# Operands moved by 32 bytes, queue orders and buffers changed, the last inverse transform in steps of two pairs: a spectral layer with a feed-forward network

## The chip, the cores and the metric

The kernel runs on one core of a Trainium2 chip. TensorE (PE) multiplies matrices; its weight loads (PEld) are shown apart. VectorE (DVE), ScalarE (ACT) and GpSimd (POOL) work elementwise, and SyncE (SP) issues the DMAs. TensorE writes into PSUM, which has eight banks; all else lies in SBUF, at a byte offset that is the same in each of 128 partitions. The metric is device time of one execution in microseconds (us); smaller is better.

## The reference

A spectral layer over 8 sequences of 3008 rows and 256 channels, then a two-layer network on all 24064 rows:

```python
def _attn_ref(x, w_r, w_i, b_r, b_i):
    X = np.fft.rfft(x, axis=1)
    Xr, Xi = X.real, X.imag
    Yr = Xr @ w_r - Xi @ w_i + b_r
    Yi = Xr @ w_i + Xi @ w_r + b_i
    Yr = np.sign(Yr) * np.maximum(np.abs(Yr) - lam, 0.0)     # lam = 0.01
    Yi = np.sign(Yi) * np.maximum(np.abs(Yi) - lam, 0.0)
    return np.fft.irfft(Yr + 1j * Yi, n=x.shape[1], axis=1)

def _moe_ref(x, w_in, w_out):        # x: 24064 x 256, w_in: 256 x 2048, w_out: 2048 x 256
    h = x @ w_in
    return (h - np.tanh(h)) @ w_out
```

## The kernel before

**The mathematics.** The transform of 3008 = 64 x 47 points is split: a DFT over 47 points (class `Forward`, L216 to L218), one over 64 points (`Spectrum`, L262), the linear layer (L289, products `ps_t` and `ps_v`), the shrinking step, an inverse over 64 points (L336 to L338), and an inverse over 47 points (class `Unit`, L428), which gives the rows of the network's input in `raw`. A sequence has 32 pairs of residues; a pair becomes 94 rows. Values are kept as a high and a low part (`x_h`, `x_l`) in a rounded 32-bit format, and a product is three matmuls: high by low, high by high, low by high. `split_into` makes the parts: ScalarE casts the high one (L87) and GpSimd, or VectorE at the start, subtracts (L88). The matmuls of L262 and L428 take plain 32-bit operands, and the profile shows each as two records.

**The network.** The rows are cut into 48 chunks of 512 or 480 columns. Chunks 0 to 2 (`Chunk.up`, L481, and `Chunk.down`, L505) run while the weights are still being unpacked. From chunk 3 on, `Pair` makes two blocks of 128 hidden units at a time with seven half-size products instead of eight (L576, three matmuls each, 256 or 240 columns), from operands `y_...` and from weights `win` or sums of weights `sum...`; between the products ScalarE copies (L584, L585) and VectorE adds (L592 `u3`, L598 `low_right`). Then come tanh (L607), the difference (L610), the high part `gh` (L614) and the low part `gl` (L618), and the down-projection, L505: twelve matmuls a pair with `wout` as weights and `gh`, `gl` as the moving operand, 512 or 480 columns wide. One pair is two slots of the plan.

**What sets the order.** The order on each engine is written out by hand. `plan()` puts each piece of spectral work into a slot with a rank; `run(slot)` issues a slot's pieces by rank. DFT over 64 points: rank 6; `shared` and `cross` products: 4 and 3; shrinking and inverse: 2; the split of x: 2, one slot ahead of `Forward.part`, which is rank 7; the operands of the next chunk (four of them in the third slot before it): 1; a `Unit` step: 8; weight sums and sums of operands: 9. Engines then run their own queue strictly in this order and wait for each other by semaphores. Work of VectorE and GpSimd that follows a piece is returned by it and issued a little later (`run_later`).

**Buffers.** Spectral work of the main loop shares two PSUM banks (`ps_ff`, in `bank()`). A `Unit` loads up to three pairs, and `time(t)` multiplies them for one half `t` of the channels into one bank and copies it out: four steps a chunk. A chunk's first rows may belong to the unit of the chunk before; they wait in `spill` until `unspill`. `weight_sums` makes the sums of weights in four steps on VectorE, in three small tiles `ws0` to `ws2`, from which ScalarE and GpSimd split them; it runs at slots 36 to 53, where the early chunks end and the pairs begin. Before the loop the pools `ps_h`, `ps_o` and `ps_f` hold eight banks; they are closed, and `ps_oo`, `ps_ff` and `ps_e` take them.

**Places.** A partition's offsets are given out in order of the pools and tags. The tile `shifts` (two columns, for two constants of activations) and what lies around it leave every later tile at byte 32 of a 64-byte block, `gh`, `gl`, `th`, `x_h`, `x_l`, `z_h`, `z_l`, `raw` and the `y` operands among them; `win` and `wout`, ahead of it, are at multiples of 64.

## Time and profile before

| | |
|---|---|
| median of three runs | 2660.9 us (2659.74 to 2662.64) |
| the profiled execution's own time | 2656.65 us |
| its span, first to last instruction | 2654.8 us |
| mean granted clock of TensorE | 0.994 |
| DMA | 163.90 MB, mean 62 GB/s |

The profile is of one execution. A row of the timeline has start and length in us, engine, line, operation, out<-in, shape, and in brackets the idle time before it with what ended it. A row of a group has the count after x, then busy us, mean ns of one, and idle us before them with their releasers. Matmuls are pipelined: a matmul's length is longer than the distance to the next one's start, so the pace is read from starts. A row of windows has the stretch and its length, busy us of the engine, the granted clock, and the DMA share. Idle time of an engine that nobody waits for costs nothing.

### The profile page before, as it was taken

How to read it: one execution, taken by the hardware profiler on the slowest of the kernel's cores; microseconds unless marked ns; L12 is line 12 of the kernel's file. 1: busy time of each engine (PE TensorE's matmuls, PEld its weight loads, DVE VectorE, ACT ScalarE, POOL GpSimd, SP SyncE). 2: the span in 40 equal slices, each digit the busy share in tenths (PEclk: the TensorE clock that was granted, in tenths of full speed). 3: DMA queues.
4: the chain of work that ended last, by engine and by line, in shares of the span. 5: the costliest groups of instructions: out<-in, count | busy, mean ns of one | idle time of the engine just before them, and what ended most of it. 6: DMA issues, size and time to landing. Idle time of an engine off the chain costs nothing.

```text
span 2654.8 us, 43312 instructions
## 1 busy us (share of the span) xinstructions
PE 2611.6 (98%) x16641; PEld 2343.2 (88%) x16641; DVE 1720.6 (65%) x2613; ACT 1578.9 (59%) x2950; POOL 697.9 (26%) x829
## 2 busy tenths in 40 slices
PE   8999999999999999999999999999999999999999
PEld 6787788899989999899998999989999899999998
DVE  6787676576656667466664666646665566665655
ACT  5555656655566555755566555665556655555555
POOL 0002524322242222512334232332223322221210
PEclk8899999999999999999999999999999999999999
DMA  6420313211131111311114011231112211111000
GB/s 195 149 76 14 110 59 102 70 40 53 38 111 55 47 50 40 106 59 40 45 49 125 29 54 38 73 95 41 43 52 84 68 46 55 36 33 33 16 24 16
DMA packets 104654, 163.90 MB, mean 62 GB/s; under 512 B 8000, under 2 KB 62272, under 8 KB 104352
## 3 DMA queue, kind: packets, MB, share of 16 engines
q1 hardware_dynamic: 104448, 161.13, 19.7%
q8 instruction: 132, 2.16, 0.3%
q14 instruction: 74, 0.61, 0.1%
HBM read 86.13 MB, written 74.97 MB: 61 GB/s over the span
## 4 chain that ended last, share of the span: by engine, by line
PE 86%; DVE 2%; POOL 1%; ACT 1%; issue 1%; DMA 0%; SPq 0%; POOLq 0%; ACTq 0%; DVEq 0%
PE o L505 36%; PE H L576 32%; PE ps_v L289 4%; PE ps_i L428 4%; PE ps_f L262 3%; PE ps_t L289 2%; PE ps_f L218 1%; PE ps_f L216 1%; PE ps_f L217 1%; DVE y L326 1%; PE ps_i L336 1%; PE ps_i L337 1%; PE ps_i L338 1%; POOL x_l L88 1%; DVE tb L300 0%
## 5 line engine op out<-in xcount | busy, mean ns | idle before, releaser
L576 PEld LDWEIGHTS H<-y_t,sum 128*128 128x128 f32 x3240 | 530.6, 188 | 91.8 <-DVE H L592 3.9
L505 PE MATMUL o<-gh,wout_l 128*128 128x512 f32 (+1 forms) x1440 | 572.5, 398 | 0.1
L505 PE MATMUL o<-gh,wout_h 128*128 128x512 f32 (+1 forms) x1440 | 561.5, 390 | 0.0
L505 PE MATMUL o<-gl,wout_h 128*128 128x512 f32 (+1 forms) x1440 | 560.7, 389 | 0.5 <-DVE gl L618 0.5
L576 PE MATMUL H<-y_t,sum 128*128 128x256 f32 (+1 forms) x3240 | 550.9, 278 | 4.1 <-DVE H L592 3.5
L614 ACT CAST gh<-th 128x1024 fp32r<-128x1024 f32 (+1 forms) x360 | 372.3, 1034 | 281.1 <-DVE th L610 231.4
L618 DVE TENSOR_TENSOR gl<-th,gh 128x1024 fp32r<-128x1024 f32 (+1 forms) x360 | 435.7, 1210 | 48.8 <-ACT gh L614 44.1
L592 DVE TENSOR_TENSOR H<-H,late 128x256 f32<-128x256 f32 (+1 forms) x360 | 153.6, 427 | 450.5 <-PE H L576 407.7
L610 DVE TENSOR_TENSOR th<-H,th 128x1024 f32<-128x1024 f32 (+1 forms) x360 | 429.3, 1192 | 2.4 <-ACT th L607 0.3
L607 ACT ACTIVATE th<-H 128x1024 f32<-128x1024 f32 (+1 forms) x360 | 364.6, 1013 | 108.8 <-PE H L576 105.7
L505 PEld LDWEIGHTS o<-gl,wout_h 128*128 128x128 f32 x1440 | 270.3, 188 | 56.1 <-DVE gl L618 0.9
L88 POOL TENSOR_TENSOR z_l<-mn,z_h 128x512 fp32r<-128x512 f32 x84 | 110.3, 1313 | 769.3 <-ACT z_h L87 769.3
L598 DVE TENSOR_TENSOR H<-H,late 128x256 f32<-128x256 f32 (+1 forms) x360 | 153.6, 427 | 242.1 <-PE H L576 235.7
L576 PE MATMUL H<-y_b,win_h 128*128 128x256 f32 (+1 forms) x1440 | 284.7, 279 | 0.0
L505 PEld LDWEIGHTS o<-gh,wout_l 128*128 128x128 f32 x1440 | 272.1, 189 | 6.8 <-ACT gh L614 0.5
L505 PEld LDWEIGHTS o<-gh,wout_h 128*128 128x128 f32 x1440 | 272.0, 189 | 5.7
L584 ACT COPY late<-H 128x256 f32<-128x256 f32 (+1 forms) x360 | 132.8, 369 | 235.5 <-PE H L576 232.6
L576 PE MATMUL H<-y_more,win_h 128*128 128x256 f32 (+1 forms) x1440 | 266.5, 278 | 0.0
L576 PEld LDWEIGHTS H<-y_more,win_h 128*128 128x128 f32 x1440 | 219.0, 189 | 4.4
L576 PEld LDWEIGHTS H<-y_b,win_h 128*128 128x128 f32 x1440 | 219.6, 189 | 0.0
L576 PE MATMUL H<-y_more,win_l 128*128 128x256 f32 (+1 forms) x720 | 209.3, 291 | 0.0
L576 PE MATMUL H<-y_b,win_l 128*128 128x256 f32 (+1 forms) x720 | 200.8, 279 | 0.0
(173 smaller groups left out, 4213.6 us busy)
## 6 DMA issues: line engine op xcount, KB each, us to landing
xt<-in_x SPq DMA_DIRECT2D x64, 384.0 KB, 3.8
at<-a SPq DMA_DIRECT2D x96, 256.0 KB, 3.2
z<-zo SPq DMA_DIRECT2D x96, 256.0 KB, 2.1
a<-st SPq DMA_DIRECT2D x56, 384.0 KB, 3.4
zin<-z SPq DMA_DIRECT2D x58, 288.0 KB, 3.8
out<-ot SPq DMA_DIRECT2D x32, 512.0 KB, 3.1
out<-ot SPq DMA_DIRECT2D x16, 480.0 KB, 3.4
zin<-z SPq DMA_DIRECT2D x31, 192.0 KB, 3.6
```

The source lines that it names most:

```text
L88: rest.tensor_tensor(out=lo, in0=src, in1=hi.bitcast(F32), op=ALU.subtract)
L289: nc.tensor.matmul(dst, lhs[:, t], rhs[:, t, :], start=n == 0, stop=n == 5)
L428: nc.tensor.matmul(ps[:, k * 94:(k + 1) * 94], self.zt[:, k, t * P:(t + 1) * P], i2t[:, (self.p + k) * 94:(self.p + k + 1) * 94], start=Tr ...
L505: nc.tensor.matmul(self.o[t][:, :n], lhs[:, f, t * P:(t + 1) * P], rhs, start=f == 0 and k == 0, stop=f == NF - 1 and k == 2,)
L576: nc.tensor.matmul(dst, a, b, start=start and k == 0, stop=k == 2, skip_group_check=True)
L584: nc.scalar.copy(out=self.p7, in_=self.c11)
L592: nc.vector.tensor_tensor(out=self.c21, in0=self.acc, in1=self.p7, op=ALU.add)
L598: nc.vector.tensor_tensor(out=self.c22, in0=self.acc, in1=self.p7, op=ALU.add)
L607: nc.scalar.activation(out=self.th, in_=self.hp[:, :, :n], func=AF.Tanh)
L610: nc.vector.tensor_tensor(out=self.th, in0=self.hp[:, :, :self.n], in1=self.th, op=ALU.subtract)
L614: nc.scalar.copy(out=self.gh, in_=self.th)
L618: nc.vector.tensor_tensor(out=self.gl, in0=self.th, in1=h(self.gh), op=ALU.subtract)
```

## The change

**Places.** The tile `shifts` becomes `below` with one column; `rebias` is made later, by GpSimd instead of VectorE, as a tile of the pool `work` of its own, just ahead of the tag `ot`. All tiles from `ot` on move up by 32 bytes, to multiples of 64: `gh`, `gl`, `th`, `raw`, `st`, and the tiles of `x_h`, `x_l`, `z_h`, `z_l`, `xh`, `xl`, `s_h`. What lies ahead of it stays: the `y` operands, `sum...`, `at`, `zin`, the constants.

**Queue orders.** The split of x goes from rank 2 to 0.5, ahead of the operands. The inverse over 64 points goes from rank 2 to 2.5, and to 6.5 where its slot holds a DFT (6) and nothing of ranks 3, 4, 7, 8. `Unit` steps are placed by `unit_slots`, first into slots whose only spectral work is a DFT. And the memory of `rebias` is set on GpSimd.

**Buffers.** `weight_sums` has two tiles with two parts each: steps three and four put the second sum into a fourth part instead of overwriting one that is being split. The PSUM pools open in the order `ps_f`, `ps_h`, `ps_o`, so that the early chunks' pool `ps_e` takes the banks of `ps_h` and `ps_o` instead of those of `ps_f`; and `ps_e` waits tile by tile for the banks' last users.

**Units.** A unit loads up to four pairs, and `both(k)` does two pairs for both halves into one bank, with one copy for both: three steps a chunk instead of four. The matmuls are the same in number and shape.

```diff
+    ps_f = start.enter_context(tc.tile_pool(name="ps_f", bufs=4, space=PSUM))
     ps_h = start.enter_context(tc.tile_pool(name="ps_h", bufs=2, space=PSUM))
     ps_o = start.enter_context(tc.tile_pool(name="ps_o", bufs=1, space=PSUM))
-    ps_f = start.enter_context(tc.tile_pool(name="ps_f", bufs=4, space=PSUM))
...
-                self.zt = work.tile([96, 3, D], F32, name="zin", tag=tag, bufs=1)
+                self.zt = work.tile([96, 4, D], F32, name="zin", tag=tag, bufs=1)
...
-        def multiply(self, ps, t):
-            for k in range(self.n):
+        def multiply(self, ps, t, at=0, which=None):
+            for j, k in enumerate(which or range(self.n)):
...
+        def both(self, k):
+            ps = bank("ps_i2")
+            m = min(2, self.n - k)
+            n = m * 94
+            for t in range(2):
+                self.multiply(ps, t, t * n, range(k, k + m))
+            pv = ps[:, :2 * n].rearrange("p (t n) -> p t n", t=2)
+            for chunk, at, cols in self.pieces(k, m):
+                chunk.take_both(at, pv[:, :, cols])
...
+        def take_both(self, at, src):
+            nc.scalar.copy(out=self.home(at, src.shape[2]), in_=src)
...
-        t = [work.tile([P, 2, P], F32, name=f"ws{k}", tag="tmp", bufs=4) for k in range(3)]
+        pair = [work.tile([P, 2, 2, P], F32, name=f"ws{k}", tag="tmp", bufs=4) for k in range(2)]
+        t = [v[:, k] for v in pair for k in range(2)]
...
         def three():
             put_sum(0, t[1])
-            op(t[1], t[1], t[2], ALU.subtract)
+            op(t[3], t[1], t[2], ALU.subtract)
             whole(t[2], 1, 0)
 
         def four():
-            put_sum(1, t[1])
-            op(t[2], t[2], t[1], ALU.subtract)
+            put_sum(1, t[3])
+            op(t[2], t[2], t[3], ALU.subtract)
...
     def run(slot):
-        for _, _, fn, a in sorted(slots.pop(slot, []), key=lambda e: e[:2]):
+        events = slots.pop(slot, [])
+        ranks = {e[0] for e in events}
+        if ranks >= {2.5, 6} and not ranks & {3, 4, 7, 8}:
+            events = [(6.5, *e[1:]) if e[0] == 2.5 else e for e in events]
+        for _, _, fn, a in sorted(events, key=lambda e: e[:2]):
...
-                (k + shrink, 2, lambda s=s: [s.shrink], 0.3), (k + inverse, 2, s.inverse, 0.7),
+                (k + shrink, 2, lambda s=s: [s.shrink], 0.3), (k + inverse, 2.5, s.inverse, 0.7),
...
-        put(slot - 1, 2, f.split, q)
+        put(slot - 1, 0.5, f.split, q)
...
-            at = (zs - 8, zs - 7, zs - 6, zs - 6) if c == WB_N else calmest(zs - 10 if i == 0 else zs - 14, zs - 6, 4, 0.7)
-            for k, (p, n) in enumerate(((lo, 3), (lo + 3, hi - lo - 3))):
+            at = unit_slots(c, (hi - lo + 1) // 2)
+            for p, first in ((lo, 0), (lo + 4, 2)):
...
+                put(max(at[first] - 5, done_at.get(b, 0) + 1, last_two[-3] + 1), 0, u.load)
+                for k in range(0, n, 2):
+                    put(at[first + k // 2], 8, u.both, k)
...
+        alone = [k for k in range(lo, hi + 1) if {e[0] for e in slots.get(k, ())} & {2, 2.5, 3, 4, 6, 7} == {6}]
+        found = alone[:n]
...
-        shifts = const.tile([P, 2], F32, name="shifts")
-        below, rebias = shifts[:, 0:1], shifts[:, 1:2]
+        below = const.tile([P, 1], F32, name="below")
         nc.vector.memset(below, -LAM)
-        nc.vector.memset(rebias, -896.0)
...
+        rebias = work.tile([P, 1], F32, name="rebias", bufs=1)
+        nc.gpsimd.memset(rebias, -896.0)
...
-        ps_e = first_pass.enter_context(tc.tile_pool(name="ps_e", bufs=1, space=PSUM))
+        ps_e = first_pass.enter_context(tc.tile_pool(name="ps_e", bufs=1, space=PSUM, reuse_waits="tile"))
```

What it does to three queues. First GpSimd, three slots before a chunk from one of the later sequences begins: `y_t` and `y_b` are low parts of the chunk's operands, `x_6_0_l` that of the sixth forward piece, `late` and `raw` sums of operands. Before:

```order
L531 TENSOR_TENSOR late<-raw 128x256
L531 TENSOR_TENSOR raw<-raw 128x256
L531 TENSOR_TENSOR late<-raw 128x256
L88 TENSOR_TENSOR y_t_1981<-late,y_t_1981 128x256
L88 TENSOR_TENSOR y_b_1982<-raw,y_b_1982 128x256
L88 TENSOR_TENSOR y_t_1984<-late,y_t_1984 128x256
L88 TENSOR_TENSOR y_b_1983<-raw,y_b_1983 128x256
L88 TENSOR_TENSOR x_6_0_l<-xt,x_6_0_h 94x512
```

And now:

```order
L550 TENSOR_TENSOR late<-raw 128x256
L550 TENSOR_TENSOR raw<-raw 128x256
L550 TENSOR_TENSOR late<-raw 128x256
L88 TENSOR_TENSOR x_6_0_l<-xt,x_6_0_h 94x512
L88 TENSOR_TENSOR y_t_1980<-late,y_t_1980 128x256
L88 TENSOR_TENSOR y_b_1981<-raw,y_b_1981 128x256
L88 TENSOR_TENSOR y_t_1983<-late,y_t_1983 128x256
L88 TENSOR_TENSOR y_b_1982<-raw,y_b_1982 128x256
```

The split of x stands ahead of the four operands now; the casts on ScalarE move in the same way.

Second TensorE, in a slot of the second sequence's spectra (`z_6` goes through the inverse, `at` through the DFT; `H` belongs to the pair that the slot lies in). Before:

```order
L576 MATMUL H_2036<-y_b_1982,win_h 128x240 x2
L336 MATMUL ps_i_3381<-z_6_h,i_l 128x512
L337 MATMUL ps_i_3381<-z_6_h,i_h 128x512
L338 MATMUL ps_i_3381<-z_6_l,i_h 128x512
L262 MATMUL ps_f_3388<-f_126,at 128x2x64 x4
L576 MATMUL H_2035<-y_more,win_l 128x240
```

And now:

```order
L595 MATMUL H_2035<-y_b_1981,win_h 128x240 x2
L262 MATMUL ps_f_3373<-f_125,at 128x2x64 x4
L336 MATMUL ps_i_3383<-z_6_h,i_l 128x512
L337 MATMUL ps_i_3383<-z_6_h,i_h 128x512
L338 MATMUL ps_i_3383<-z_6_l,i_h 128x512
L595 MATMUL H_2034<-y_more,win_l 128x240
```

The DFT goes ahead of the inverse in seven of the ten slots that hold both; the other three hold a `Unit` step too.

Third VectorE, in a round of weight sums (`the`, `gle` and `he` belong to the early chunks). Before, step three overwrites `ws1`, which GpSimd is reading:

```order
L631 TENSOR_TENSOR ws1_1850<-ws0_1849,ws1_1850 128x256
L631 TENSOR_TENSOR ws0_1849<-ws2_1851,ws0_1849 128x256
L490 TENSOR_TENSOR gle_1058<-the_1054,ghe_1056 128x512
L485 TENSOR_TENSOR the_1053<-he0_1049,the_1053 128x512
L631 TENSOR_TENSOR ws1_1850<-ws1_1850,ws2_1851 128x256
L628 TENSOR_TENSOR ws2_1851<-win_h_78,win_l_79 128x256
```

And now it writes the second part of `ws1` while the second part of `ws0` is read:

```order
L651 TENSOR_TENSOR ws0_1850<-ws0_1850 128x256
L651 TENSOR_TENSOR ws0_1850<-ws1_1851,ws0_1850 128x256
L509 TENSOR_TENSOR gle_1059<-the_1055,ghe_1057 128x512
L504 TENSOR_TENSOR the_1054<-he0_1050,the_1054 128x512
L651 TENSOR_TENSOR ws1_1851<-ws0_1850,ws1_1851 128x256
L648 TENSOR_TENSOR ws1_1851<-win_h_78,win_l_79 128x256
```

The order is the same; the buffers differ, and with them what has to be waited for.

More of the change, by code (lines that the diff above doesn't have):

```diff
@@ L438, in take @@
                 end = min(hi, begin[c] + sizes[c])
-                src = ps[:, lo - self.b * S - self.p * 94:end - self.b * S - self.p * 94]
-                chunks[c].take(t, lo - begin[c], src, c)
+                yield chunks[c], lo - begin[c], slice(lo - first, end - first)
                 lo = end
+        def take(self, ps, t):
+            for chunk, at, cols in self.pieces():
+                chunk.take(t, at, ps[:, cols])
+        def both(self, k):
[7 more added lines that the diff above has]
+                chunk.take_both(at, pv[:, :, cols])
     Unit.turn = 0
@@ L456, in open, with take @@
                 )
-        def take(self, t, at, src, c):
+        def take(self, t, at, src):
             n = src.shape[1]
@@ L763, in plan, with unit_slots @@
             zs = zero_slot(c)
-            at = (zs - 8, zs - 7, zs - 6, zs - 6) if c == WB_N else calmest(zs - 10 if i == 0 else zs - 14, zs - 6, 4, 0.7)
-            for k, (p, n) in enumerate(((lo, 3), (lo + 3, hi - lo - 3))):
-                u = Unit(b, p, n)
-                put(max(at[2 * k] - 4 + k, done_at.get(b, 0) + 1), 0, u.load)
-                for t in range(2):
-                    put(at[2 * k + t], 8, u.time, t)
+            at = unit_slots(c, (hi - lo + 1) // 2)
+            for p, first in ((lo, 0), (lo + 4, 2)):
+                n = min(4, hi - p)
+                if n <= 0:
+                    continue
+                u = Unit(b, p, n)
+                last_two.append(at[first + (n - 1) // 2])
+                put(max(at[first] - 5, done_at.get(b, 0) + 1, last_two[-3] + 1), 0, u.load)
+                for k in range(0, n, 2):
+                    put(at[first + k // 2], 8, u.both, k)
+    last_two = [0, 0]
+    def unit_slots(c, n):
+        zs = zero_slot(c)
+        if c == WB_N:
+            return (zs - 8, zs - 7, zs - 6)
+        lo, hi = (zs - 10 if c % WB_N == 0 else zs - 14), zs - 6
+        alone = [k for k in range(lo, hi + 1) if {e[0] for e in slots.get(k, ())} & {2, 2.5, 3, 4, 6, 7} == {6}]
+        found = alone[:n]
+        rest = [k for k in range(lo, hi + 1) if k not in found]
+        found = sorted(found + sorted(rest, key=lambda k: (load_at.get(k, 0.0), k))[:n - len(found)])
+        for k in found:
+            busy(k, 0.9)
+        return found
     wsteps = {}
```

22 lines of the change are left out of this document (12 added, 10 removed).

## The prediction

> **What bounds the kernel now.** I read the page first, for the engine that sets the end, then the chain of work, then the matmuls grouped by shape, then the list of waits, and last the timeline at the places where TensorE waits.
>
> ```profile
> span 2654.8 us, 43312 instructions
> PE 2611.6 (98%) x16641; PEld 2343.2 (88%) x16641; DVE 1720.6 (65%) x2613; ACT 1578.9 (59%) x2950; POOL 697.9 (26%) x829
> ...
> PE 86%; DVE 2%; POOL 1%; ACT 1%; issue 1%; DMA 0%; SPq 0%; POOLq 0%; ACTq 0%; DVEq 0%
> ```
>
> TensorE (PE) is busy 98% of the span, and 86% of the chain that ended last is its own matmuls; no other engine passes 65%. So two things can shorten the span: matmuls that follow each other faster, and TensorE's waits, 2654.8 - 2611.6 = 43 us in all. The list of waits says for whom:
>
> ```profile
> PE ps_f L218 <- POOL x_l L88: 9.8, 7, 1.6
> PE ps_f L262 <- DVE y L326: 7.2, 10, 0.7
> PE H L576 <- DVE H L592: 3.5, 1, 3.5
> ...
> PE H L481 <- DVE the L485: 1.7, 1, 1.7
> PE he L481 <- DVE yl L462: 1.6, 1, 1.6
> ...
> PE H L576 <- POOL y_b L88: 0.7, 1, 0.7
> ```
>
> Columns: us in total, times, longest. These six rows are 24.5 us, and each is touched by an edit. Busy time says little of how fast matmuls follow each other, since they overlap; that is read from their starts, in steps of the timeline where nothing waits:
>
> ```profile
> 1.91 5.06 PE L815 MATMUL idle<-warm 128*128 128x512 f32 x11 [1.91 <-DVE shifts L821]
> ...
> 105.44 1.99 PE L815 MATMUL idle<-warm 128*128 128x512 f32 x8
> ...
> 1108.84 0.38 PE L505 MATMUL o<-gh,wout_l 128*128 128x480 f32 x1
> ...
> 1110.16 0.50 PE L576 MATMUL H<-y_t,sum 128*128 128x240 f32 x3
> ...
> 2408.44 0.40 PE L505 MATMUL o<-gh,wout_l 128*128 128x512 f32 x1
> ...
> 2409.84 0.52 PE L576 MATMUL H<-y_t,sum 128*128 128x256 f32 x3
> ```
>
> Between the two rows at 2408.44 and 2409.84 stand six L505 matmuls of 512 columns: 1.40 / 6 = 0.233 us each. With 480 columns, from 1108.84 to 1110.16, it is 1.32 / 6 = 0.220. The eight idle matmuls at 105.44, one set of weights and nothing accumulated, take (1.99 - 0.40) / 7 = 0.227. The eleven at 1.91, at half the granted clock, take (5.06 - 0.79) / 10 = 0.427, if their last runs twice 0.40 (the same 0.43 as at 281.96 below, after the clock has dropped). Half of 0.427 is 0.2135: what 512 columns cost if the clock alone set the pace. So at the full clock a matmul of 512 columns loses 13 ns when alone and 19.5 ns in the loop, which it does not lose at the half clock. That looks like operand reading, not like a fixed number of clock cycles. All of them start at byte 32 of a 64-byte block.
>
> **The change part by part.** All sums are against the profiled execution's own 2656.65 us; the median of the three runs, 2660.9, is 4.25 above it, and that is added at the end.
>
> *Operands moved by 32 bytes.* The count, from the page, the groups by shape and the source lines:
>
> ```profile
> L505 PE MATMUL o<-gh,wout_l 128*128 128x512 f32 (+1 forms) x1440 | 572.5, 398 | 0.1
> ...
> L505 PE MATMUL o<-ghe,wout_h 128*128 128x512 f32 x64 | 25.3, 395 | 0.0
> ...
> L218 PE MATMUL ps_f<-x_l,f_h 94*96 94x512 f32 x112 | 44.9, 401 | 10.0 <-POOL x_l L88 9.8 <-DVE x_l L88 0.2
> ...
> L338 PE MATMUL ps_i<-z_l,i_h 128*128 128x512 f32 x84 | 33.1, 394 | 0.0
> ```
>
> Each stands for a group of three products: 3 x (1440 + 64 + 112 + 84) = 5100 matmuls whose moving operand now starts at a multiple of 64 (gh, gl, x_h, x_l, z_h, z_l); some 200 in smaller groups are left out. The operands of L576 stay at 32. No matmul at this rate in the trace starts at a multiple of 64, so the price has two far ends: below, the whole 19.5 ns go, 99 us; above, a loss of as much. I take one block's time: 2048 bytes that start inside a block touch 33 blocks and not 32, and a block is 0.2135 / 32 = 6.7 ns. That is half of what the idle row loses (13 ns), the nearest row, since nothing else can disturb it. 5100 x 6.7 ns = **-34 us**.
>
> *The x split ahead of the operands (rank 0.5).* Once in each of six batches POOL makes four y operands first, and x_l late:
>
> ```profile
> 1109.04 0.74 POOL L88 TENSOR_TENSOR y_t<-late,y_t 128x256 fp32r<-128x256 f32 x1 [1.50 <-PE H L576]
> 1109.73 0.74 POOL L88 TENSOR_TENSOR y_b<-raw,y_b 128x256 fp32r<-128x256 f32 x1
> ...
> 1111.83 2.18 POOL L88 TENSOR_TENSOR x_l<-xt,x_h 94x512 fp32r<-94x512 f32 x1
> ...
> 1111.50 0.28 PE L576 MATMUL H<-y_b,win_l 128*128 128x256 f32 x1
> ...
> 1114.06 0.47 PE L218 MATMUL ps_f<-x_l,f_h 94*96 94x512 f32 x1 [1.58 <-POOL x_l L88]
> ```
>
> Moved first, x_l takes the place of the first y_t, from about 1109.2 (its cast is 0.2 us longer). At 1.3 us, the usual length, it ends 1.8 us before TensorE reaches it (1112.3: from 1111.50 three L576, then L216 and L217). The 9.8 us go. Late next are the y operands: y_t ends near 1111.2, and its low part is read at 1111.4; y_b ends near 1111.95 and is read at 1111.73 (third matmul from 1111.50). That is 0.25 us of new waiting, 6 times: 1.5. The two y splits behind them are read four microseconds later and hide. **-8.3 us**.
>
> *Inverse behind the DFT (rank 6.5).* In the new queue of TensorE it applies in seven of the ten slots that wait; three hold a Unit too and keep their order.
>
> ```profile
> 355.33 1.71 DVE L326 TENSOR_TENSOR y<-tb,ps_v 64x256 f32<-64x256 f32 x4
> ...
> 355.44 0.47 PE L336 MATMUL ps_i<-z_h,i_l 128*128 128x512 f32 x1
> ...
> 357.10 1.16 PE L262 MATMUL ps_f<-f,at 128*128 128x128 f32 x8 [0.72 <-DVE y L326]
> 358.10 0.80 PE L428 MATMUL ps_i<-i,zin 96*128 96x94 f32 x6
> ```
>
> Both need a bank, and one of the two banks is free only when y is added, at 357.04. Now: 355.44 to 358.10, 2.66 us. Then: the DFT first (1.0 us), a wait until 357.10, three inverse matmuls of 0.23: 2.35. So the wait moves to the inverse and only 0.3 us is won, 7 times: **-2.1 us**.
>
> *Weight sums with a fourth buffer.* In each of the four weight steps a DVE operation no longer waits for POOL to read what it overwrites:
>
> ```profile
> 277.19 1.48 DVE L631 TENSOR_TENSOR ws<-ws,ws 128x256 f32<-128x256 f32 x1 [3.13 <-POOL sum L88]
> 278.71 2.05 DVE L628 TENSOR_TENSOR ws<-win_h,win_l 128x256 f32<-128x256 f32 x1
> 280.68 0.42 DVE L592 TENSOR_TENSOR H<-H,late 128x256 f32<-128x256 f32 x1
> ...
> 281.15 1.01 PE L576 MATMUL H<-y_t,sum 128*128 128x256 f32 x3 [3.48 <-DVE H L592]
> 281.96 0.63 PE L505 MATMUL o<-gh,wout_l 128*128 128x512 f32 x1
> 282.39 0.63 PE L505 MATMUL o<-gh,wout_h 128*128 128x512 f32 x1
> ...
> 284.00:285.00 1.00, 1.00 (x7) 0.83 0.00 0
> ```
>
> L631 starts 3.1 us sooner, so L592 does, and 0.5 of the 3.5 us is left: -3.0. After the wait the clock is halved (0.43 between starts at 281.96); the 0.83 granted from 284 to 285 means a third of that microsecond, so until 284.34: 3.2 us at half speed, -1.6. The same cause delayed L485 (1.7) and then y_b (0.7): -2.2. **-6.8 us**.
>
> *PSUM pools in another order.* The first L481 group no longer takes banks that L462 still reads, so the 1.6 us row goes: **-1.6 us**. ps_e by tile adds no wait, since its banks were idle before.
>
> *Units of four pairs, both halves in one bank.* TensorE does the same matmuls:
>
> ```profile
> L428 PE MATMUL ps_i<-i,zin 96*128 96x94 f32 x1024 | 142.3, 275 | 2.9 <-DMA zin<-z 2.3 <-ACT st L230 0.7
> L469 ACT COPY raw<-ps_i 128x282 f32<-128x282 f32 x88 | 35.2, 400 | 48.1 <-PE ps_i L428 47.7
> ```
>
> Copies of this kind on ScalarE fall from 254 to 174 in the built programs, under TensorE's matmuls (ScalarE is 59% busy): nothing. If that cover failed, the steps would wait for a bank, some 0.4 us (one copy) each. A DFT slot now often holds a step too; what is queued behind is the cast of gh, pushed back by one copy (0.4), while TensorE itself is 0.9 us later (8 matmuls). Loads grow by a third; the first of batch 1 already comes late (part of the 2.3 us): **+1.0 us**.
>
> Sum without the addresses: -8.3 - 2.1 - 6.8 - 1.6 + 1.0 = -17.8. With them -52: 2656.65 - 52 + 4.25 = **2609 us**.
>
> **The rivals.**
>
> *The start address changes nothing* (a repeated cost inside the stream, not its start): 2656.65 - 17.8 + 4.25 = **2643**. For it: the loss is about as large a share at 256 columns as at 512, as a cost all along the stream would be. From 2411.26 to 2411.61 three L576 matmuls of 256 columns take 0.117 each, 10 ns over half of 0.2135.
>
> ```profile
> 2411.26 0.28 PE L576 MATMUL H<-y_b,win_l 128*128 128x256 f32 x1
> ...
> 2411.61 0.28 PE L576 MATMUL H<-y_more,win_l 128*128 128x256 f32 x1
> ```
>
> The Trainium skill (SBUF — State Buffer, section "Door 1: The DMA port swizzle") speaks for this rival: it gives SBUF lines of 16 bytes, and starts of 32 and 0 are both multiples of 16, so by that rule the edit would save nothing of the 34 us. No run here shows such a line.
>
> *The start costs in every block*, so that the idle row's whole 13.1 ns goes: 67 us in place of 34, **2576**. For it: the same proportional loss, read the other way. The Trainium skill (TensorE: Matmul & The Clock Gate, section "Wait — 56ns, not 53.3ns?") has starts N / 2.4 GHz + 2.5 ns apart, 215.7 ns for 512 columns; the idle row's 227 differs, and by this rule 11 of the 13 ns would be there to win, 2587.
>
> *Slower: moving operand and weights now start at the same place in a block* (wout is at a multiple of 64 already), and the two reads of one matmul get in each other's way. At one block each, +34 us: 2656.65 - 17.8 + 34 + 4.25 = **2677**. It decides from 17.8 us / 5100 = 3.5 ns a matmul. Against it: L576 has an equal and an unequal pair of places today, sum at byte 32 and win at byte 0 beside y at byte 32. From 2409.84 to 2410.20 three with sum take 0.120 each, no better and no worse than the 0.117 with win above.
>
> ```profile
> 2410.20 0.40 PE L505 MATMUL o<-gh,wout_l 128*128 128x512 f32 x1
> ```
>
> *The waits only move* (each removed wait is found again at the next reader, as at the inverse) and the address does nothing. Then only the L462 row and the half clock, 1.6 each, are won: 2656.65 - 3.2 + 4.25 = **2658**. For it: ten of the removed waits are for y, which is not made sooner.
>
> **How the numbers follow.** Forecast 0.55 (2609; its own range 2587 to 2628, as the block's cost is 3 to 11 ns). Nothing from addresses 0.24; in every block 0.08; waits only move 0.06; slower 0.07. The range is 2573 to 2652: it takes in the first three and leaves out the last two, 0.13, and a little of the edges. About 0.2% (5 us) is what a measurement of this kernel can tell from no change. Faster by more: 0.55 + 0.24 + 0.08 = 0.87; within: 0.06; slower: 0.07.
>
> **What would show it.** Right: six L505 matmuls in a row at 1.36 us, not 1.40, and the shares of L216 to L218 and L336 to L338 down alike, with L576 still 0.117; the L218, L592, L485 and L462 rows gone from the waits; L336 waiting for y about 0.6 us seven times; no half clock after 281. Wrong: L505 still at 0.233, or above it; new rows for y_b at chunk starts longer than 0.3 us, or for banks at L428. The prediction falls if the L505 spacing moves by other than 3 to 11 ns.

## The result and the profile after

The changed kernel takes 2636.06 us (median of four runs, 2633.25 to 2638.48), beside 2661.08 for the kernel before on the same chip: a ratio of 0.9909, 95% interval 0.9898 to 0.9921, which is 24 us less by the ratio and 25 by the medians. The forecast was 2609, so the direction and the range held and the size did not: 24 us of 52. The nearest of the cases was the rival "the start address changes nothing", 2643.

The profiled execution took 2638.48, the longest of the four, while that of the kernel before was shorter than its median; so the traces lie 18 us apart and not 24. In the program after, L505 stands at L524, L576 at L595, L481 at L500, L592 at L611 and L485 at L504; L216 to L428 kept their numbers. The page's first part and the chain's shares by engine:

```profile
span 2636.7 us, 43245 instructions
PE 2604.5 (99%) x16641; PEld 2344.8 (89%) x16641; DVE 1728.6 (66%) x2612; ACT 1571.5 (60%) x2870; POOL 695.5 (26%) x830
...
PE 92%; issue 2%; POOL 2%; DVE 2%; DMA 1%; ACT 1%; POOLq 0%; SPq 0%; ACTq 0%; DVEq 0%
```

PE's busy time fell by 7.1 us (2611.6 before) and the span by 18.1, so 11 us of the gain are idle time of PE that went. The list of waits (us in total, times, longest) says which:

```profile
PE ps_f L262 <- DMA at<-a: 4.1, 1, 4.1
PE ps_i L336 <- DVE y L326: 4.0, 7, 0.6
PE ps_i L428 <- DMA zin<-z: 3.6, 2, 2.3
...
PE ps_f L262 <- DVE y L326: 2.2, 3, 0.7
...
PE ps_f L218 <- POOL x_l L88: 0.9, 2, 0.5
...
PE H L595 <- POOL y_t L88: 0.6, 4, 0.2
...
PE H L500 <- DVE the L504: 0.3, 1, 0.3
```

The wait for x_l fell from 9.8 to 0.9 us, those for the weight sums (L592, 3.5) and for yl (1.6) are gone, the one for `the` fell from 1.7 to 0.3. Seven waits for y moved from L262 to L336. Two rows for loads grew; before they were:

```profile
PE ps_f L262 <- DMA at<-a: 2.4, 1, 2.4
...
PE ps_i L428 <- DMA zin<-z: 2.3, 2, 1.1
```

The wait for `at` lies at the start of the kernel (34 us) and varies from trace to trace (2.5 us in e3, 4.3 in e10). The other is for the first steps of batch 1. The timeline there:

```profile
441.70 1.99 PE L428 MATMUL ps_i<-i,zin 96*128 96x94 f32 x8 [2.26 <-DMA zin<-z]
```

and the windows behind it (busy time of each engine, with the granted clock third number from the end):

```profile
441.00:445.00 4.00, 3.30 (x15) 3.33 (x16) 0.00 (x0) 1.05 (x2) 0.37 (x1) 0.56 0.69 200
445.00:448.00 3.00, 3.00 (x12) 2.72 (x11) 0.40 (x2) 1.48 (x2) 1.27 (x1) 0.50 0.08 29
```

The wait of 2.26 us is followed by half clock until 448. Last, the down-projection where nothing waits, and the new start of a chunk:

```profile
2391.15 0.28 PE L595 MATMUL H<-y_b,win_l 128*128 128x256 f32 x1
...
2391.50 0.39 PE L524 MATMUL o<-gh,wout_l 128*128 128x512 f32 x1
...
2392.88 0.51 PE L595 MATMUL H<-y_t,sum 128*128 128x256 f32 x3
...
1100.19 1.29 POOL L88 TENSOR_TENSOR x_l<-xt,x_h 94x512 fp32r<-94x512 f32 x1 [1.69 <-ACT x_h L87]
1101.45 0.73 POOL L88 TENSOR_TENSOR y_t<-late,y_t 128x256 fp32r<-128x256 f32 x1
1102.14 0.73 POOL L88 TENSOR_TENSOR y_b<-raw,y_b 128x256 fp32r<-128x256 f32 x1
...
1102.57 0.74 PE L595 MATMUL H<-y_b,win_h 128*128 128x256 f32 x2
...
1103.62 0.40 PE L218 MATMUL ps_f<-x_l,f_h 94*96 94x512 f32 x1
```

Six L524 in a row take 1.38 / 6 = 0.230 us (0.233 before; the forecast wanted 0.227), three L595 of 256 columns (2391.50 - 2391.15) / 3 = 0.117, as before. At the chunk's start x_l is ready long before 1103.62, and the second of the two y_b matmuls waits for y_b: two take 0.74 and not 0.39.

Over the whole trace (mean distance from one start to the next, at the full clock, without those followed by a wait): 512 columns of the down-projection 235.6 before and 233.0 after, 480 columns 220.1 and 219.9, 256 columns of the up-projection 118.4 and 118.1, L216 to L218 unchanged. Part of that is not pace. A matmul that follows a plain 32-bit one (L428 or L262) starts only 28 to 59 ns behind the last record of that one, and the matmul after it comes some 316 ns later at 512 columns; with fewer Unit steps there are 79 such distances among those of 512 columns, where there were 114. Without them the means are 232.5 before and 230.9 after at 512 columns, 218.4 and 218.8 at 480, 117.2 and 117.4 at 256. So of these the 512-column matmuls alone became faster, by 1.6 ns.

### The profile page after: what moved, and what is told of

Read it like the earlier page. It is cut to its first block, busy times and chain, and to the rows that moved or that the text cites. A ratio compares the mean times of both kernels' runs of the same rounds, so it can differ in the third digit from the quotient of the medians.

```text
span 2636.7 us, 43245 instructions
## 1 busy us (share of the span) xinstructions
PE 2604.5 (99%) x16641; PEld 2344.8 (89%) x16641; DVE 1728.6 (66%) x2612; ACT 1571.5 (60%) x2870; POOL 695.5 (26%) x830
## 4 chain that ended last, share of the span: by engine, by line
PE 92%; issue 2%; POOL 2%; DVE 2%; DMA 1%; ACT 1%; POOLq 0%; SPq 0%; ACTq 0%; DVEq 0%
PE o L524 37%; PE H L595 32%; PE ps_v L289 4%; PE ps_i L428 4%; PE ps_f L262 3%; PE ps_t L289 2%; PE he L500 2%; PE ps_v L371 1%; PE ps_f L218 1%; PE ps_f L216 1%; PE ps_f L217 1%; DVE y L326 1%; PE oe L524 1%; PE ps_i L336 1%; PE ps_i L337 1%
## 5 line engine op out<-in xcount | busy, mean ns | idle before, releaser
L595 PEld LDWEIGHTS H<-y_t,sum 128*128 128x128 f32 x3240 | 531.3, 189 | 86.9 <-POOL y_t L88 1.4
L524 PE MATMUL o<-gh,wout_l 128*128 128x512 f32 (+1 forms) x1440 | 568.5, 395 | 0.1
L524 PE MATMUL o<-gl,wout_h 128*128 128x512 f32 (+1 forms) x1440 | 560.2, 389 | 0.5 <-DVE gl L637 0.5
L524 PE MATMUL o<-gh,wout_h 128*128 128x512 f32 (+1 forms) x1440 | 559.8, 389 | 0.0
L595 PE MATMUL H<-y_t,sum 128*128 128x256 f32 (+1 forms) x3240 | 551.0, 278 | 1.4 <-ACT ot L535 0.7
L637 DVE TENSOR_TENSOR gl<-th,gh 128x1024 fp32r<-128x1024 f32 (+1 forms) x360 | 441.3, 1226 | 58.1 <-ACT gh L633 54.4
L611 DVE TENSOR_TENSOR H<-H,late 128x256 f32<-128x256 f32 (+1 forms) x360 | 153.5, 426 | 417.9 <-PE H L595 373.9
L524 PEld LDWEIGHTS o<-gl,wout_h 128*128 128x128 f32 x1440 | 270.9, 188 | 55.3 <-DVE gl L637 0.9
L595 PE MATMUL H<-y_b,win_h 128*128 128x256 f32 (+1 forms) x1440 | 286.4, 279 | 0.5
L524 PEld LDWEIGHTS o<-gh,wout_l 128*128 128x128 f32 x1440 | 272.2, 189 | 9.1 <-DVE ot L537 1.1
L524 PEld LDWEIGHTS o<-gh,wout_h 128*128 128x128 f32 x1440 | 271.9, 189 | 6.7
L595 PE MATMUL H<-y_more,win_h 128*128 128x256 f32 (+1 forms) x1440 | 267.4, 279 | 0.4 <-POOL y_more L88 0.4
L595 PEld LDWEIGHTS H<-y_more,win_h 128*128 128x128 f32 x1440 | 220.0, 189 | 5.9 <-POOL y_more L88 0.6
L595 PEld LDWEIGHTS H<-y_b,win_h 128*128 128x128 f32 x1440 | 219.6, 189 | 1.7 <-POOL y_b L88 1.7
L595 PE MATMUL H<-y_more,win_l 128*128 128x256 f32 (+1 forms) x720 | 206.4, 287 | 0.5 <-DVE H L617 0.5
L595 PE MATMUL H<-y_b,win_l 128*128 128x256 f32 (+1 forms) x720 | 200.1, 278 | 0.0
```

Source lines behind the costliest of these rows:

```text
L524: nc.tensor.matmul(self.o[t][:, :n], lhs[:, f, t * P:(t + 1) * P], rhs, start=f == 0 and k == 0, stop=f == NF - 1 and k == 2,)
L595: nc.tensor.matmul(dst, a, b, start=start and k == 0, stop=k == 2, skip_group_check=True)
L611: nc.vector.tensor_tensor(out=self.c21, in0=self.acc, in1=self.p7, op=ALU.add)
L637: nc.vector.tensor_tensor(out=self.gl, in0=self.th, in1=h(self.gh), op=ALU.subtract)
```

## The experiments

Theory at the start: the addresses bring some 7 us, the queue orders and buffers some 18. The rivals: the forecast (34 from the addresses), and nothing from them. All ratios are to the kernel before, run beside it on the same chip, with 95% intervals; one per mille is 2.7 us. Kernels with rows behind their end do the whole computation first.

**e1, addresses alone** (on the kernel before)

```diff
-        shifts = const.tile([P, 2], F32, name="shifts")
+        below = const.tile([P, 1], F32, name="below")
...
+        rebias = work.tile([P, 1], F32, name="rebias", bufs=1)
+        nc.gpsimd.memset(rebias, -896.0)
```

> The kernel before with the address edit alone (the second constant moved behind the other tiles). The forecast's step, one block of 6.7 ns for each of 5100 matmuls: -34 us, a ratio of 0.987 to before. New theory, from the traces of before and after (512-column matmuls of the down-projection start 233.0 and not 235.6 ns apart, 480 columns unchanged): about -7 us, 0.997. Addresses do nothing: 1.000. The down-projection's spacing at 512 columns would be 229, 233 and 235.6 ns in turn.

Measured: 2655.66 us, 0.9982 (0.9973 to 0.9991), 4.7 us less (2.4 to 7.2); 233.8 ns at 512 columns. The new theory fits; the forecast's 34 are excluded, and so is nothing. Here the order of the matmuls is that of before: without the distances behind plain 32-bit ones, 512 columns went from 232.5 to 230.7 ns and 480 columns from 218.4 to 218.8. For 3072 and 1536 matmuls that is 5.5 us won and 0.6 lost.

**e2, all but the addresses** (the two lines of e1 undone on the changed kernel)

> The changed kernel with the address edit undone (both constants in one tile as before), all else as changed. The forecast's step: the addresses carried more than the whole gain, so this is slower than before by some 9 us, a ratio of 1.003. New theory: addresses 7 us, the rest 18 us, so 2643 us beside a before of 2661, a ratio of 0.993. Addresses do nothing: the same time as the changed kernel, 0.991.

Measured: 2639.74 us, 0.9921 (0.9908 to 0.9935). 21 us come from the queue orders and buffers, where the forecast's sum had 17.8, and some 3 from the addresses. Its 512-column matmuls are at 232.5 ns again, without those behind plain 32-bit ones.

**e3, everything at 64** (on the changed kernel)

```diff
+        rebias = const.tile([P, 1], F32, name="rebias")
+        nc.vector.memset(rebias, -896.0)
...
-        rebias = work.tile([P, 1], F32, name="rebias", bufs=1)
-        nc.gpsimd.memset(rebias, -896.0)
```

> The changed kernel with each of the two constants in a tile of its own, so that the y operands, their sums and the other tables start at a multiple of 64 bytes too. The forecast's step (a block of 6.7 ns for each start inside a block): 5800 more matmuls of 256 and 240 columns gain 39 us, 2597. New theory (a small effect that only long matmuls show): within 4 us of the changed kernel, 2636. If equal places of weights and moving operand hurt: slower than the changed kernel, by 5 us or more.

Measured: 2629.35 us, 0.9880 (0.9865 to 0.9895): 7 us faster than the changed kernel, more than the new theory allowed and a fifth of the forecast's 39. Its trace shows about half of the 7 us as pace (512 columns 232.5 ns beside 233.0, 480 columns 218.9 beside 219.9, 240 columns 113.3 beside 113.7, 256 columns no better); the rest was not traced.

**e4, start places by themselves.** Rows of 24 matmuls behind the kernel's end: `matmul(ps, win_h[:, 0, hold:hold + 128], win_l[:, 0, move:move + 512])`.

> The changed kernel, and behind its end rows of 24 matmuls with constant operands, whose moving operand starts 0, 4, 8, 16, 32 or 48 bytes into a 64-byte block, with weights at 0 or 32, once alone (one set of weights, nothing accumulated), once as in the down-projection (weights change, six accumulate), and both with ScalarE and VectorE copying beside them. The forecast's step: 6.7 ns less at 0 than at 32, in every row. New theory: no difference alone (the idle matmuls take 227 ns at 32 in the trace before and at 0 in the trace after), 2 to 3 ns only where weights change or other engines read and write beside it. Addresses do nothing: no row differs by over 0.5 ns. Only the probed rows count, not the time.

Measured, ns from start to start in the second half of a row, 512 columns:

```
weights at 0,  moving operand at 0   4   8  16  32  48 bytes: 226.7 236.7 233.3 231.7 233.3 233.3
weights at 32, moving operand at 0  32 bytes:                 233.3 226.7
sums of three products, changing weights, 0/0, 32/0, 32/32:   226.7 233.3 226.7
the same with ScalarE copying beside, 0/0, 32/0:              226.7 233.3
480 columns, 0/0 and 32/0: 216.7 220.0;  256 columns: 120.0 117.8
```

VectorE's additions waited for nothing and ran from 2630 to 2689 us, so beside the rows of the first two lines and not where they were meant to. All three expectations fell. Some 6.7 ns are there, with constant operands too, but they hang on whether moving operand and weights start at the same place, not on where the moving operand starts: 32 with 32 is as good as 0 with 0. The forecast's yardstick, the idle matmuls, had both in one tile and so at the same place already. And equal places are worse at 256 columns. At equal places, in some rows, the first seven or so take 225 to 236 ns before 226.7 is reached.

**e5, groups of unlike lengths** (the same matmuls, groups of 512 and 256 columns taking turns)

> The changed kernel, and behind its end rows in which groups of 512-column matmuls take turns with groups of 256 columns (6 and 6, 3 and 3, 6 and 3, 12 and 12), each with the moving operand of the wide ones and of the narrow ones 0 or 32 bytes from the weights' place in a 64-byte block; ahead of them rows of 512 columns alone with 0, 64, 128, 256 and 32 bytes. Theory of settling: equal places reach 226.7 ns only after some seven matmuls of one length, so in groups of six the wide ones take 230 to 232 at equal places and about 233 at unequal ones, in groups of twelve 228 to 229, and in groups of three nothing is gained. If settling plays no part (what eats the gain is the other engines or something else of the loop): 226.7 at equal and 233.3 at unequal places in every row. 64, 128 and 256 bytes read as 0 by both. Only the rows count, not the time.

Measured: 226.7 ns at 0 and at 256 bytes between the places, 228.8 at 64, 232.6 at 128 and 233.3 at 32: 256 bytes read as 0, and 64 and 128 do not, against the expectation. The wide matmuls at equal places take 232.2 in groups of three, 231.2 in groups of six and 229.0 in groups of twelve; with both at 32 they take 232.3, 231.5 and 233.3, with 32 for the wide and 0 for the narrow 233.7, 233.6 and 233.6, with 0 for the wide and 32 for the narrow 234.4, 232.8 and 228.7. In groups of three to six at most 2 ns are left of the 6.7: in these rows short groups do keep the gain from being reached.

**e6, the x split first, alone** (on the kernel before)

```diff
-        put(slot - 1, 2, f.split, q)
+        put(slot - 1, 0.5, f.split, q)
```

> The kernel before with rank 0.5 for the x split alone. The forecast's step: 9.8 us of waits for x_l go and 1.5 us of waits for y_b come, -8.3 us, a ratio of 0.9969 to before. If the waits only move to the y operands: 1.000, with rows for y_t or y_b of 1 us and more.

Measured: 2647.14 us, 0.9951 (0.9937 to 0.9965), 13 us less. In its list of waits little is left of x_l:

```profile
PE ps_f L218 <- POOL x_l L88: 0.3, 1, 0.3
```

Its span is 9.4 us shorter than before's, near the 8.3 forecast. The other 3 to 4 fit a cost that the profiled execution of before does not have and others do. The same wait in it and in the execution of e9, where the wait is untouched, in the timeline and the window behind it, first before:

```profile
1754.17 0.47 PE L218 MATMUL ps_f<-x_l,f_h 94*96 94x512 f32 x1 [1.59 <-POOL x_l L88]
```

```profile
1755.00:1758.00 3.00, 3.00 (x20) 2.73 (x20) 1.21 (x2) 2.36 (x5) 1.81 (x3) 1.00 0.00 0
```

and e9:

```profile
1758.15 0.48 PE L218 MATMUL ps_f<-x_l,f_h 94*96 94x512 f32 x1 [1.58 <-POOL x_l L88]
```

```profile
1759.00:1762.00 3.00, 3.00 (x13) 2.79 (x13) 0.00 (x0) 2.33 (x5) 1.30 (x3) 0.50 0.00 0
```

After the same 1.6 us, full clock in one and half clock in the other (20 against 13 matmuls in 3 us). The traces of e1, e7 and e9 hold two each of such stretches of 3.4 us after a wait for x_l, at some 1.7 us each; the profiled execution of before holds none. The clocks of all executions agree: 0.992 to 0.995 in the 21 of before that ran beside e6, 0.995 or 0.996 in the five of e6.

**e7, the fourth buffer alone** (on the kernel before; `ws` in two tiles of two halves, `t[3]` for the second difference)

> The kernel before with the fourth buffer of the weight sums alone. The forecast's step: the waits at 277 to 284 and what they delay, with the half clock behind them, -6.8 us, a ratio of 0.9974. If the waits only move: the half clock alone, -1.6 us, 0.9994.

Measured: 2657.35 us, 0.9990 (0.9981 to 0.9999), 2.7 us less. The row for L592 is gone from its waits and that for L485 is 0.2, but some seven us further on a new wait stands: a Unit's step for a bank from which ScalarE has still to copy a DFT (not another Unit, as the next expectations put it). Half clock follows (timeline, then window):

```profile
288.48 1.59 PE L428 MATMUL ps_i<-i,zin 96*128 96x94 f32 x6 [1.67 <-ACT st L230]
```

```profile
288.00:292.00 4.00, 3.52 (x14) 3.39 (x15) 1.29 (x3) 2.16 (x5) 0.73 (x1) 0.55 0.37 100
```

**e9, the Units alone** (the classes Unit and Chunk and the planner's last loop as changed, on the kernel before)

> The kernel before with the new Units alone (loads of four pairs, steps of two pairs and both halves, their own choice of slots). The forecast's step: +1.0 us, 1.0004, nothing that a measurement tells from no change. Rival, from the trace after: the wait of 2.3 us for the first load of batch 1 at 441 us is followed by half clock until 448 us, so +3 to +4 us, 1.0013. Rival on the other side: fewer copies on ScalarE let it start the casts of gh sooner, and short waits in the stream of matmuls shrink, -3 us, 0.999.

Measured: 2659.86 us, 0.9999 (0.9990 to 1.0008): the forecast's "nothing that can be told".

**e8, no swap of the inverse** (on the changed kernel)

```diff
-        if ranks >= {2.5, 6} and not ranks & {3, 4, 7, 8}:
-            events = [(6.5, *e[1:]) if e[0] == 2.5 else e for e in events]
```

> The changed kernel with the inverse ahead of the DFT in every slot, as before; all else as changed. The forecast's step: the swap wins 0.3 us at seven places, so 2 us more than the changed kernel, a ratio to before of 0.9917. By the traces before and after: the waits at L262 fall by 6.2 us and those at L336 rise by 5.1, so 1 us, 0.9913. If the swap matters more than the waits show: 0.993 or above.

Measured: 2636.26 us, 0.9907 (0.9891 to 0.9922); the same as with the swap. Inconclusive between 0 and 2 us; what it excludes is the third case, 0.993 or above. Its waits are those of before again, ten for y at L262:

```profile
PE ps_f L262 <- DVE y L326: 7.2, 10, 0.7
```

**e13, three buffers again** (on the changed kernel)

> The changed kernel with three buffers for the weight sums, as before; all else as changed. The forecast's step: 6.8 us lost, a ratio to before of 0.9935. By the run with the fourth buffer alone (a ratio of 0.999): 2.8 us lost, 0.992. If the parts help each other (in that run the wait that went at 281 us came back as 1.8 us at 288 us, for a bank that the old Units hold, with half clock behind it, and with the new Units it does not): 5 us or more, 0.993 and above.

Measured: 2640.09 us, 0.9922 (0.9910 to 0.9935), 3.5 us more than the changed kernel's ratio; the interval does not tell 2.8 from 6.8. The trace has L611 waiting 3.5 us and L500 1.9, and 10.2 us of half clock at 249 and 273 that the changed kernel lacks. It also shows a shorter start by chance (4 us), so no figure is drawn from it alone.

**e11, the same place in 256 bytes** (on e3: the constant's tile with 56 columns in place of 1)

> The changed kernel with a padding of 192 bytes ahead of all tables, so that each moving operand and its weights start at the same place of a 256-byte block (the changed kernel: 64 bytes apart in the down-projection, 32 in the up-projection; with everything at 64: 64 apart in both). Theory from the rows of 24 (226.7 ns at 0 or 256 bytes apart, 228.9 at 64, 232.9 at 128, 233.3 at 32) with settling, which leaves less than half of it in groups of three to six: 1 ns for each of some 4500 matmuls of 512 and 480 columns less than with everything at 64, so some 4 us below that kernel's 2629: 2625, a ratio of 0.987. If 64 bytes are enough: 0.988. If places count for nothing in the loop: the changed kernel's 0.991.

Measured: 2640.17 us, 0.9927 (0.9914 to 0.9939). The theory from the rows fell: 11 us slower than e3, and by 5 us slower than the changed kernel, which the overlapping intervals do not make certain. Its trace has 119.5 ns at 256 columns (118.3 in e3), which the 120 of e4 had shown and the expectation left out, and 233.9 at 512 (232.5), where 1 ns less was expected. For 4872 and 3072 matmuls that is 5.8 and 4.3 us, about the whole difference.

**e12, and a later first step** (on e11)

```diff
-            return (zs - 8, zs - 7, zs - 6)
+            return (zs - 7, zs - 6, zs - 6)
```

> The kernel with the same place in 256 bytes, and the first steps of batch 1 one slot later (slots 7, 6 and 6 ahead of the chunk in place of 8, 7 and 6). Theory: the wait of 2.3 us for the load at 441 us goes, and the 3 to 7 us of half clock behind it, so 4 to 5 us less than the kernel without it: 2621, 0.985. Rival: the next reader waits as long (the zin load, or a bank for two steps in one slot): no difference, 0.987.

Measured: 2639.30 us, 0.9920 (0.9906 to 0.9934). The wait for the load is 0.3 us and the half clock is gone, yet the difference of 0.9 us is inside the intervals.

**e10, the same edit on e3**

> The changed kernel with everything at a multiple of 64 bytes, and the first steps of batch 1 one slot later. By the trace of the same edit on the kernel with the same place in 256 bytes (its loop was 4.2 us shorter): 4 us below everything at 64 alone, 2625, a ratio of 0.9865 to before. If the wait only moves: 0.988.

Measured: 2630.27 us, 0.9892 (0.9876 to 0.9909), no gain that can be told. Between 436 and 452 the clock is full throughout, as the row of its busiest stretch shows, so the wait did go; what it costs over many executions is below what these runs tell.

```profile
440.00:444.00 4.00, 3.72 (x27) 3.24 (x25) 2.25 (x3) 3.53 (x8) 1.77 (x2) 1.00 0.41 112
```

**e14, the loop's own order of groups**

> The changed kernel, and behind its end rows that repeat the loop's own order of groups (12 of 256 columns, 3 of 512, 6 of 256, 6 of 512, 3 of 256, 3 of 512), four times each, with 0, 32, 64, 96, 128, 160, 192 and 224 bytes between the places of moving operand and weights, and some mixed pairs. If distance and group length alone explain the loop: the mean over a round is lowest at 64 for both (as with everything at 64), higher at 64 for the wide with 32 for the narrow (the changed kernel) by 0.3 to 0.6 ns a matmul, at 32 for both (before) by 1 ns, at 0 for both by 1.2 ns. If not, the order of the rows differs from that of the four kernels, and something else of the loop decides. Only the rows count.

Measured, us for a round of 33 matmuls from the second round on, at 0, 32, 64, 96, 128, 160, 192 and 224 bytes: 5.273, 5.260, **5.127**, 5.320, 5.273, 5.273, 5.207, 5.273; wide at 64 with narrow at 32: 5.233, with narrow at 0: 5.320. The order is that of four kernels: e3, the changed one, e2 (the places of before) and e11, at 0.9880, 0.9909, 0.9921 and 0.9927. The intervals of the last three overlap, and in the first three kernels the products with `sum` are 0 bytes apart and those with `win` are not, which no row repeats. The rows lie 3 to 4 ns a matmul above the one at 64, not 0.3 to 1.2. At 64 the narrow ones take 113.3 ns and the wide ones 228.8.

**e15 and e16, everything at 64 apart** (on e10: unused tiles of 192 and 64 bytes ahead of and behind the homes of the sums; in e16 also around the transforms' operands)

```diff
+        def pad(n):
+            work.tile([P, n], F32, name=f"pad{len(pads)}", tag=f"pad{len(pads)}", bufs=1)
+            pads.append(n)
```

> The kernel with everything at a multiple of 64 bytes and the later first step, with paddings of 192 and 64 bytes that put the sums of weights 64 bytes behind the y operands they meet (they stood at the same place), so that every matmul of up- and down-projection has 64 bytes between the places. If the rows tell what the kernel does: 256 columns from 118.3 to 114 or 115 ns (4872 matmuls, -18 us) and 512 columns from 232.4 to about 230 (3072, -7 us), so some 25 us less: 2605, a ratio to before of 0.980. If the loop is bound by something else as well: within 5 us of the kernel without the paddings, 0.988.

> As the run before, with two more paddings (64 and 192 bytes) that put 64 or 192 bytes between the places in the transforms and the spectral products too (1512 matmuls of 256 columns from 119.7 to 115 or so, -6 us; 670 of 512 columns, -2 us): 8 us below the run before, 2597, a ratio of 0.977. If places count for nothing there: the same as the run before.

Measured: e15 2629.22 us, 0.9889 (0.9874 to 0.9903), so nothing of the 25 us; its trace has 118.3 and 232.7 ns, where e10 has 118.3 and 232.4. What the rows promised, the loop did not give. e16 2624.19 us, 0.9867 (0.9850 to 0.9883), the fastest kernel of the study, with 118.0 in place of 120.0 ns in the spectral products; by the ratios it is 6 us below e15, of 8 expected, with intervals that overlap.

**e17, what the rows lack**

> The changed kernel, and behind its end the rows in the loop's order, at 64 and at 32 bytes between the places, with constant operands, with changing weights, with changing weights and moving operands, with four banks and sums of three products, with all three, and with all three while ScalarE and VectorE copy beside them. At 64 bytes the constant row takes 113.3 ns at 256 columns and 228.8 at 512, the loop 118 and 232.5. Whichever addition brings the row from the first pair to the second is what takes the gain from the kernel. If none does: what is left is that TensorE's instructions wait for semaphores in the loop, and no row can show it. Only the rows count.

Measured from the second round on: at 64 bytes 5.127 us a round with constant operands, changing weights, changing moving operands, four banks, and all three; 5.260 (118.0 and 231.9 ns, close to the pair that the expectation gives for the loop) in the last row alone. At 32 bytes 5.260 in all six rows. VectorE's additions ran beside the first two rows, which kept 5.127; beside the last rows only ScalarE's copies ran.

**e18, copies beside or the beginning**

> The changed kernel, and behind its end the rows in the loop's order with constant operands, 64 bytes apart: alone; begun by one more matmul of 512 or of 256 columns into another bank and nothing else; the same with 32 copies by ScalarE from that bank, with 8 (a quarter of the row), with copies by ScalarE from SBUF, with 24 copies by VectorE from that bank; and three rows at 192 bytes, alone, with copies, alone. If the copies take the gain: 113.3 and 228.8 ns in all rows without copies, 118 and 232 in those with, and in the row of 8 copies the first round alone is slow. If the beginning decides (two rhythms that each keep themselves): the row begun by one matmul is slow without copies too, and a slow row stays slow to its end when the copies have stopped. Only the rows count.

Measured, us a round from the second on, at 64 bytes, in the order of the run:

```
alone                                        5.127
begun by one matmul of 512 columns           5.260
begun by one matmul of 256 columns           5.220
begun by 512, 32 copies by ScalarE beside    5.127   (copies from 2699.03 to 2718.81, the whole row)
alone                                        5.127
begun by 512, 8 copies (first quarter)       5.260   all four rounds
begun by 512, ScalarE copying from SBUF      5.260
alone                                        5.260
begun by 512, 24 copies by VectorE           5.260
alone                                        5.260
at 192 bytes, alone, with 32 copies, alone   5.227  5.207  5.207
```

The copies do not take the gain: the row with 32 of them is fast, and a row without any is slow. The same 132 matmuls at the same places go in at least three rhythms (sequences of distances that repeat), and from the second round on a row keeps its own to the end; the rows "alone" behind another at 64 bytes took that of the row ahead. One matmul of 512 columns ahead is not enough to name the rhythm either: behind a row of 5.127 or of 5.260 it led to 5.260 (four rows here), behind the row of 5.220 to 5.127 (one row, the one with 32 copies). The last row of e17 at 64 bytes, begun the same way behind 5.127, had 5.260 too. No two rows with the same rhythm ahead and the same beginning differ. At 32 bytes only 5.260 was seen, in seven rows, which are not all the ways to begin one. The reading that fits all this is that the distance sets which rhythms exist and that what went before picks one; it was not tested beyond these rows. That also limits e5 and e14: their rows are one pick each.

## Why the prediction was wrong in size

*Operands moved by 32 bytes (-34).* This step failed: 34 us were charged and 3 to 5 came (e2, e1). That a quiet row does show 6.6 ns between equal places and 32 bytes is luck. The forecast made its 6.7 from one more block of 64 bytes at an unaligned start, and e4 has 226.7 ns with both operands at byte 32, and 10 ns of loss at 4 bytes. Three things in the step were wrong. It tied the price to the start of the moving operand, while e4 shows the distance to the weights; by the tiles' offsets the edit turned 32 bytes of distance into 64 for the down-projection, 0 into 32 for L217, L218 and L336 to L338, and left the up-projection at 32 with `win` and at 0 with `sum`. It charged 5100 matmuls alike, while in the down-projection only those of 512 columns gained, 1.8 ns in e1 and 1.6 in the changed kernel, and those of 480 lost 0.4. And it took the rate of an undisturbed row for groups of three to six, where (e18) the rhythm depends on what ran before. In which rhythm the loop runs was not followed: without the distances behind plain 32-bit matmuls, the means of e3 and e15 are 117.5 and 117.6 ns at 256 columns and 230.3 and 230.5 at 512, near those of the rows of 5.220 (117.7 and 229.1) and 5.260 (118.0 and 231.9), and far from the fast 113.3 at 256. In e15 nothing more was won, though in both projections all distances were 64. What in the chip makes the rhythms stays open.

The step also reads the eleven idle matmuls at 1.91 us as run at half the granted clock. The profile's window from 2 to 7 us has a clock of 1.00; half clock is read from their pace, 0.427 us, which is that of the matmuls at 281.96, where the clock did fall. The base of 0.2135 us stands by those.

The condition under which the prediction falls, a spacing that moves by other than 3 to 11 ns, was met: 1.6. Its rival "nothing" fell too, by e1, and with it "in every block"; "the waits only move" fell by e2, 21 us without the addresses. "Slower" fell in its stated form: equal places are the fast ones at 512 columns. The price of that rival does appear at 256 (120.0 against 117.8), and in e11 it is about half of the loss.

*The x split (-8.3).* Right in mechanism and in the trace: 9.8 us became 0.9, and the new wait for y_b is 0.24 us six times, as forecast (0.25). As a term it was too small, 13 us in e6 (9 to 17). The reason that fits is that the sum was made against one execution in which no half clock followed the 1.6 us waits. The 4.25 us between that execution and the median were added at the end as if the change could not touch them; part of them seems to have been this cost: e6 ran at a granted clock of 0.995 to 0.996 beside 0.992 to 0.995. The Trainium skill (TensorE: Matmul & The Clock Gate, section "What's actually happening") has the clock set by a free-running window of about 3.4 us, which agrees with stretches of 3.4 us that follow a wait in one execution and not in the next. The same page of the Trainium skill, section "HAM oscillation — how this bites in real kernels", warns of gaps above some 3.4 us; as a limit that is too loose here, since 1.58 us were enough in e9.

*Inverse behind the DFT (-2.1).* The wait moved to L336 as worked out, seven times, 0.57 us each. The sum of both rows went from 7.2 to 6.2 us; e8 cannot tell 2 us from none.

*Fourth buffer (-6.8).* All its waits went in the changed kernel. Alone it brought 2.7 us (0.3 to 5.1), so alone the term was too large; in that trace a wait came back at L428 for a bank (e7). With the new Units that wait is absent, and e13 gives 3.5 by the ratios; within the whole change the intervals do not tell 3.5 from 6.8. That the two edits help each other fits the traces, and the ratios do not prove it.

*Units (+1.0).* Not contradicted: -0.3 with 2.4 either way (e9). The load of batch 1 was late by 2.3 us, as named, and half clock followed, which the step did not price; e10 and e12 could not measure it.

*Pool order (-1.6).* The row for yl at L481 is gone, and one of 0.4 us for yl stands at L428. It was not tried alone.

The parts alone, 4.7 + 13 + 2.7 + 0.3, make 21 of the 24 us; the inverse and the pools, not measurable or not tried, may have the rest. That the sum without the addresses came close, 17.8 for the 21 of e2, is in part luck: the x split was too small by about as much as the fourth buffer and the inverse were too large.

## What to carry to other kernels

A price read from a quiet row holds for the row; before it is multiplied by thousands, ask whether the loop ever runs long enough in one form to reach that rate, and what the row's operands have in common that the loop's have not. A wait of 1.6 us on TensorE cost about twice its length in some executions (1.7 us of half clock behind it) and not in others, so a sum made against one execution should look at the clock behind each wait in several of them. Where two edits touch neighbouring waits, try them together and apart: what one frees the other may have to let through.

## What the runs showed that was not expected

- Distance between the places of weights and moving operand, for matmuls of 512 columns from split (rounded) operands in long rows: 226.7 ns at 0 or 256 bytes, 228.8 at 64, 232.6 at 128, 233.3 at 32, 236.7 at 4. At 256 columns 0 bytes is the worse: 120.0 against 117.8 at 32.
- The same sequence of matmuls ran at 5.127, 5.220 or 5.260 us a round, depending on what ran ahead of it (the rhythm of the row before and one more matmul), and kept its rhythm through the next row (e18).
- ScalarE copying from PSUM for 19.8 us, and VectorE's copies, left the rhythm of TensorE as it was, while they ran and when they stopped (e18).
- In these traces the distance behind a plain 32-bit matmul is no pace: the next start is 28 to 59 ns behind its last record and the one after that some 316 ns further at 512 columns, so a mean over all distances moves when such neighbours become fewer.
- Shifting all tables by 192 bytes (e3 to e11) cost 11 us with not one instruction of the computation changed.
